# Down projection of the short token tiles on two column halves of the array

## The chip, the core and the metric

One core of a Trainium2 chip runs one program. The metric is the device time of the program in microseconds, the median of several executions; less is better. The engines named below are TensorE (PE; its weight loads are listed as PEld), VectorE (DVE), ScalarE (ACT), GpSimd (POOL) and SyncE (SP, which issues most DMAs).

## What is computed

A delta-rule attention over 4 batches, 8 heads, 768 tokens, whose output (4 x 768 tokens of 384 channels) goes through a mixture of 8 experts, of which each token uses one:

```python
# x: [4, 768, 384] from the attention; w1: [8, 384, 1024]; w2: [8, 1024, 384]
e = fresh_e if (s == 0 or local_gate[b, s] < 0.5) else prev_e
...
h = np.maximum(x[b, s] @ w1[e], 0.0)
out[b, s] = p[e] * (h @ w2[e])
```

The change concerns the last line, the down projection `h @ w2[e]`, for a few of the tokens.

## The kernel before

The first 440 us or so hold the attention, the routing and the mixture's expert 0 and place 1, issued in an order written out by hand. Then `Moe.rest` runs places 2 to 7: the experts other than 0, the fullest first. A place `e` has a fixed number of token slots, `CAPS[e]`, out of (480, 496, 480, 448, 416, 384, 384, 384), in tiles of 128, so that the last tile of a place can be shorter: 96 slots for place 2, 64 for place 3, 32 for place 4; places 5 to 7 have three full tiles.

Numbers are kept in two float16 parts, hi and lo, and a product is three matmuls: hi by hi, hi by lo, lo by hi.

One place goes as follows in the program, and each engine takes its instructions in this order.

- At the start the weights of the place after it are asked for: seven pieces (three of `w1`, pieces 0 to 2; four of `w2`, pieces 3 to 6), through four staging buffers on SP's queue. The tokens of the place after it are gathered on POOL (L490) and later transposed by a DMA (L842).
- Up projection: for each of 8 blocks `f` of 128 hidden channels, 9 matmuls into one of three PSUM banks `pt` (L502), with the weights as the stationary operand and the place's tokens as the columns that stream. ACT makes the hi part of `h` from the bank (`uphi`, L503), DVE a float32 copy (`upt`, L504), and DVE the lo part (L850).
- Down projection: for each token tile `j` of `m` tokens 24 matmuls (`downm`, L509) into one of two PSUM banks `po`. Here the tokens' hidden values are the stationary operand (128 channels by `m` tokens), and 384 output columns of `w2` stream. Then DVE scales the bank into a buffer `y` (`yo`, L510), and POOL scatters the rows to DRAM (L492).
- Between these, the weights of the place after it are split: ACT makes the hi part of a piece (`whi`, L485), DVE the lo part (`wlo`, L487). At tile `j` = 3 both parts of the last piece, 6, stand behind the tile's scaling. A lo part that is done frees a staging buffer, for which SP's next weight load waits.

Some work on the list of tokens that did not fit (L760 to L830) is put between tiles.

Of the kernel before, what the change touches and what calls it, by code (L numbers as in the profile page):

```python
"""Delta-rule attention followed by a top-1 mixture of experts with carried routing."""
# [13 lines left out]
class Buf:  # L15
    """a buffer of a pool, placed when its first instruction is issued"""
# [11 lines left out]
class Sched:  # L28
    """the instructions in program order, with what each reads, writes, writes a part of, and holds; issued in the order of ORDER.
    A function with a parameter gets the engine that ORDER names."""  # L30
# [19 lines left out]
class Attn:  # L50
    NKT=9; NKJ=9; NQC=2; NBD=2; GATE=1; NKF=4; NK16=2; NQV=3; NY=2; NCMP=3; NAM=1; NLX=2; NTT=1; NTX=1; NXC=1; NPO=2; NPK=1; NPT=3; AMG=()
    def __init__(s, ctx, tc, qv,k,beta,xs,wg,wl,lg):
        s.tc=tc; s.nc=nc=tc.nc; s.xs=xs
        s.qv_,s.k,s.beta=qv,k,beta
        s.NSTEP=k.shape[0]; s.NM=s.NSTEP//4
        s.wg,s.wl,s.lg=wg,wl,lg; s.sqrts=[]
        E=ctx.enter_context
        s.cp=E(tc.tile_pool(name="ac",bufs=1))
        s.pp=E(tc.tile_pool(name="ap",bufs=1,space=PSUM))
        T=lambda sh,dt,n:s.cp.tile(sh,dt,name=n)  # L60
        P=lambda n,sh,dt,nm:Pool_([T(sh,dt,f"{nm}{i}") for i in range(n)],nm)
        s.zsrc=T([128,1],F32,"zsrc")
        s.mask=T([128,32],F32,"mask")       # [(h,s),t]: 2^-6 where s<t
        s.KJ=P(s.NKJ,[128,2,8,128],F16,"KJ")       # token-major, head j of pair at column 64 j
        s.KT=P(s.NKT,[128,2,8,128],F16,"KT")       # [(j,d), z, u, (h,s)]
        s.QT=P(2,[128,2,2,8,128],F16,"QT")         # [(j,d), p, z, u, (h,t)] zero but for the heads of pair p
        s.QC=P(s.NQC,[128,2,8,2,32],F16,"QC")      # [(j,d), z, u, p, t]; the squares too
        s.bd=P(s.NBD,[128,32,128],F16,"bd")
        s.kf=P(s.NKF,[128,2,384],F32,"kf"); s.qv=P(s.NQV,[128,896],F32,"qv")
        s.bt=P(2,[128,32],F32,"bt")  # L70
        s.ss=P(2,[128,32],F32,"ss"); s.s0=P(1,[128,32],F32,"s0"); s.t0=P(1,[128,32],F32,"t0"); s.rr=P(2,[128,32],F32,"rr")
        s.k16=P(s.NK16,[128,2,2,384],F16,"k16")
        s.gt=P(1,[128,32,32],F32,"gt"); s.L=P(s.NLX,[128,1056],F32,"L"); s.X=P(s.NLX,[128,1056],F32,"X"); s.TT=P(s.NTT,[128,32,32],F32,"TT"); s.bs=P(1,[128,32],F32,"bs")
        s.ft=P(2,[128,256],F32,"ft"); s.mneg=T([128,1],F32,"mneg"); s.c64=T([128,1],F32,"c64")   # -2^-6 for the first 16 rows of a head, else 0
        s.TX=P(s.NTX,[128,16,32],F32,"TX"); s.XC=P(s.NXC,[128,2,16,32],F16,"XC"); s.GC=P(s.NXC,[128,2,32,16],F16,"GC"); s.QQ=P(1,[128,2,8,16],F16,"QQ")
        s.cmp=P(s.NCMP,[128,4,8,32],F16,"cmp"); s.am=P(s.NAM,[128,8,32],F32,"am")
        s.R=P(2,[128,4,48],F32,"R"); s.Rs=P(2,[128,2,4,48],F16,"Rs"); s.Us=P(2,[128,2,4,48],F16,"Us")
        s.y=P(s.NY,[128,2,2,384],F16,"y")
        s.Shp=P(3,[128,2,4,48],F16,"Sh"); s.Slp=P(3,[128,2,4,48],F16,"Sl")
        s.Sps=s.pp.tile([128,2,512],F32,name="Sps")  # L80
        s.po=Pool_([s.pp.tile([128,512],F32,name=f"po{i}") for i in range(s.NPO)],"po")
        s.pk=Pool_([s.pp.tile([128,512],F32,name=f"pk{i}") for i in range(s.NPK)],"pk")
        s.pt=Pool_([s.pp.tile([128,512],F32,name=f"pt{i}") for i in range(s.NPT)],"pt")
        if s.GATE:
            s.wc=T([128,3,9],F32,"wc"); s.wc16=T([128,2,3,9],F16,"wc16")
            s.xt=P(1,[128,12,128],F16,"xt")
    @staticmethod
    def blk(t,z,u,p): return t[:,p,z,u,:]
    def build(s,extra=(),post=None):
# [3 lines left out]
        # ---- constants  # L93
# [25 lines left out]
        # ---- program  # L119
# [57 lines left out]
        def K3(i,k16,k6,ii):  # L177
# [10 lines left out]
            # the keys without the zeros of the other head's rows  # L188
# [6 lines left out]
            g=s.pt()  # L195
# [14 lines left out]
        def T_(m):  # L210
            M=mac[m]; L=s.L(); X=s.X(); bs=s.bs(); TT=M["TT"]=s.TT(); gt=M["gt"]; b=M["b"]
            full=lambda t:t[:,0:1024].rearrange("p (a b)->p a b",a=32)
            dia=lambda t:t.rearrange("p (b r)->p b r",b=2)[:,:,0:512].rearrange("p b (j i)->p b j i",i=32)[:,:,:,0:16]     # both diagonal blocks: [p, block, j, i]
# [30 lines left out]
        def Q(i):  # L244
# [9 lines left out]
            for j in range(2):  # L254
                def qp(j=j):
                    q=slice(64*j,64*j+64); t=QT.t[q]; (a,_),(b,_)=t.ap[0],t.ap[1]
                    o=bass.AP(t.tensor,t.offset+32*j,[[a,64],[b+64,2],[128,16],[1,32]])      # the pair's columns lie 64 further in its own block
                    return o,QC.t[q].rearrange("r z u p c -> r p (z u) c")
                add(cp(qp),r=[QC],p=[QT]); D.setdefault('dq',[]).append(S.ops[-1])
# [20 lines left out]
        def Tc(i):  # L280
# [3 lines left out]
            # the lower left block of the inverse: - X22 G21 X11  # L284
# [30 lines left out]
        def online(i):  # L315
            D=st[i]; qv=D["qv"]; vb=lambda:qv.t[:,512:896].rearrange("p (u d) -> p u d",u=8); h_=i%2; y=D["y"]=s.y() if h_==0 else st[i-1]["y"]; KT,QT,KJ,bd=D["KT"],D["QT"],D["KJ"],D["bd"]
            for g in range(2):
                po=s.po(); pk=s.pk()
                psv=lambda po=po:po.t[:,0:384].rearrange("p (k u e) -> p k u e",k=2,u=4)      # U, y
                pkv=lambda pk=pk:pk.t[:,0:384].rearrange("r (u p e) -> r u p e",u=4,p=2)      # K S of both pairs  # L320
                bdv=lambda:bd.t.rearrange("p (k u) t -> p k u t",k=4)
                Rs=s.Rs(); Us=s.Us(); us=slice(4*g,4*g+4)
                if i>0:
                    HL=((0,(0,1)),(1,(0,)))           # the state's hi with both parts of k or q, its lo with the hi
# [71 lines left out]
        # program order of unplaced buffers does not matter: pools place them when scheduled  # L396
# [6 lines left out]
class Moe:  # L403
    CAPS=(480,496,480,448,416,384,384,384)            # slots of expert 0, then of the others, the fullest first
    SP=20; LOT=256                                    # expert 0 begins with up to LOT tokens of the first SP steps
    def __init__(s, ctx, tc, xs, lg, w1, w2, out):
        """xs [step, (b, t 32), d] in DRAM; lg [(b, t), step, logits and local logit] on chip; out [(b, t), d]"""
# [6 lines left out]
        s.NA=4*s.E+s.MO                                   # slot tiles: four of each place, then the overflow's  # L414
# [3 lines left out]
    def consts(s):  # L418
        """closures that make the constants, for the scheduler"""
        nc=s.nc; NS,E,SP=s.NS,s.E,s.SP; K=s.K  # L420
        s.ident=K([128,128],F16,"mident"); s.blk=K([128,128],F32,"blk")
        s.ones=K([128,128],F16,"ones"); s.tri=K([128,128],F16,"tri")       # tri [k,m]: 1 where k<m
# [25 lines left out]
        def f3():  # L448
# [6 lines left out]
            # key of a token: 8 (32 step + t) + 16, and 1..8 to be taken off  # L455
# [4 lines left out]
    # ---- pieces of the work  # L460
    def wsrc(s,e,k):
        """source of piece k of an expert's weights, and its shape: three of w1, four of w2"""
# [13 lines left out]
    def wv(s,t,k):  # L476
        """a piece's hi and lo, [p, hi|lo, a, b]"""
# [17 lines left out]
    def xtr(s,p,hl,m):  # L495
        """rows [m, hi|lo] -> [128 d, 6, m] in a bank"""
# [8 lines left out]
    def downm(s,po,h,W,fs,c,m):  # L505
        for f in fs:
            k=3+f//2
            for x,(a,b) in enumerate(((0,0),(0,1),(1,0))):
                s.nc.tensor.matmul(po[0:m],h(a,f)[:,c:c+m],s.wv(W[k],k)[:,b,f%2,:],start=(x==0 and f==0),stop=(x==2 and f==7))  # L509
    def yo(s,y,po,pv,m): s.nc.vector.tensor_scalar(y[0:m],po[0:m],pv[0:m],2.0**-26,op0=ALU.mult,op1=ALU.mult)  # L510
    # ---- routing, expert 0 and what place 1 starts from, as a part of the attention's schedule
    def graph(s,S,A):
# [3 lines left out]
        v=add  # L516
        # kept for the whole of the rest
# [14 lines left out]
        # weights of expert 0  # L532
# [16 lines left out]
        for z,(lo,hi) in enumerate(((0,SP),(SP,NS))):  # L549
# [15 lines left out]
            # a fresh choice where the gate, in float32, is below 0.5, and at the start  # L565
# [4 lines left out]
            # the last key so far: within a step, then over the steps  # L570
# [13 lines left out]
            # rank of a token among its expert's: the steps before, then the partitions before  # L584
            pr=A.pt(); prv=lambda pr=pr,n=n:pr.t[:,0:8*n].rearrange("p (e i) -> p e i",e=E); ptv=lambda pr=pr:pr.t[:,480:488]
            if z==0:
# [13 lines left out]
                # the others by their counts in the first steps, the fullest first: the place of each, the expert of each place, its slots  # L600
                EE=[128,E,E]; one=lambda a:a.unsqueeze(1).to_broadcast(EE); two=lambda a:a.unsqueeze(2).to_broadcast(EE)
                def f1():
# [3 lines left out]
                    V.tensor_tensor(pE,one(s.io[:,0:E]),two(s.ps),op=ALU.is_equal)       # [expert, place]  # L606
# [29 lines left out]
            if z==1:  # L636
                # a lot's second half also holds expert 0's of the first steps
# [7 lines left out]
            # softmax of the chosen expert, times 2^8, in two parts  # L645
# [9 lines left out]
            # the slots' tokens: one-hot products, 1[place] x 1[slot tile] values  # L655
# [23 lines left out]
            # the lot  # L679
# [32 lines left out]
        def f3():  # L712
            # rank, beyond the capacity, slot tile 4 place + rank / 128
# [11 lines left out]
        # place 1, and what place 2 starts from  # L725
# [48 lines left out]
    # ---- places 1.. and what did not fit  # L774
    def rest(s,A):
# [19 lines left out]
        def load(e):  # L795
            """closures: hi, lo of each piece"""
# [13 lines left out]
        def ov1():  # L810
            # tiles of 128 ranks from the capacity on, of each expert: their number, where they start
# [14 lines left out]
            # the expert of each such tile  # L826
# [17 lines left out]
        for e in range(2,E):  # L844
# [10 lines left out]
            for j in range(nj):  # L855
                m=min(128,n-128*j); po=pso()[:,0:384]; y=s.f32(yo())[:,0:384]; a=4*e+j
                s.downm(po,lambda z,f:h(z,f,n),W[e],range(8),128*j,m)
                s.yo(y,po,s.pv[:,a:a+1],m); s.scatter(y,s.so[:,a:a+1],m)
# [31 lines left out]
# the instructions of the attention and of the start of the mixture, in the order of issue; a letter names the engine where several can do it  # L890
# [111 lines left out]
def _layout(q, k, v, beta):  # L1002
    """tokens in steps of 32; batch 2 p + j, head u, chunk 4 m + c; q and v side by side"""
# [31 lines left out]
```

## Time and profile before

| | |
|---|---|
| time, median of three runs | 613.91 us (614.52, 611.40, 613.91) |
| span of the profiled execution, first to last instruction | 614.3 us |
| the profiled execution's own time | 614.52 us: the other two times are below its span |
| mean granted TensorE clock | 0.864 of full speed over the span |
| busy share of the span: PE, PEld | 77%, 60% |
| DVE, ACT, POOL | 85%, 56%, 55% |
| PE, tenths, last 12 of 40 slices | 999999999993 |
| granted clock there | 999999999997 |

A slice is 15.4 us long, and 9 stands for 90% or more. The shares mix stages with different limits: DVE has the largest share over the whole span, while in the last 12 slices PE is full and DVE's digits are 785868597650. Places 2 to 7 lie in these slices. A matmul is pipelined, and the length shown for one contains the run through the array; what one costs in a stream is read from the distance of starts.

### The profile page before, as it was taken

What the parts mean: (1) busy time and instruction counts of PE and PEld (TensorE: products, weight loads), DVE (VectorE), ACT (ScalarE), POOL (GpSimd) and SP (SyncE); (2) the same over time, 40 slices, a digit from 0 to 9 for tenths busy, and PEclk for the clock granted to TensorE, in tenths of its full rate; (3) what the DMA queues carried; (4) which work ended last, traced back from release to release, by engine and by line L of the source; (5) the groups of instructions that cost most, each with busy time, mean ns of one, the idle gap of its engine ahead of it and who ended that gap; (6) DMA issues with size and microseconds to landing.
All of it is one profiled execution on the core that took longest, in us unless ns stands there. A gap on an engine that the chain in (4) does not pass through costs nothing. (4 is left out here: it accounts for less than half of the span.)

```text
span 614.3 us, 19858 instructions
## 1 busy us (share of the span) xinstructions
PE 473.4 (77%) x8023; PEld 366.8 (60%) x8023; DVE 520.8 (85%) x1163; ACT 346.8 (56%) x745; POOL 340.8 (55%) x474
## 2 busy tenths in 40 slices
PE   0131677677789668687878769799999999999993
PEld 0131676677678667686777766654656555666661
DVE  7999998999899899989989998699785868597650
ACT  7567697678778777777878743213160605154220
POOL 7837686657667675757556764378843232414201
PEclk9998587588867777869867578799999999999997
DMA  5777777589899997797775617272567465666600
GB/s 191 129 163 119 165 99 131 93 162 169 126 164 165 131 145 127 122 161 158 121 191 118 127 40 253 70 227 89 145 209 211 127 194 170 187 162 221 120 16 29
DMA packets 244703, 88.23 MB, mean 144 GB/s; under 512 B 221651, under 2 KB 236047, under 8 KB 244608
## 3 DMA queue, kind: packets, MB, share of 16 engines
q1 hardware_dynamic: 241056, 76.87, 61.0%
q0 software_dynamic: 3552, 10.06, 5.2%
q8 instruction: 64, 1.05, 0.8%
q14 instruction: 31, 0.25, 0.2%
HBM read 46.34 MB, written 10.05 MB: 92 GB/s over the span
## 5 line engine op out<-in xcount | busy, mean ns | idle before, releaser
L502 PE MATMUL pt<-bd,KT 128*128 128x384 f16 (+4 forms) x432 | 92.0, 346 | 2.6 <-DVE tx L768 1.1
L502 PEld LDWEIGHTS <-KT 128*128 128x128 f16 x576 | 57.7, 102 | 44.3 <-issue 6.4
L201 PE MATMUL pt<-QC,KT 128*128 128x64 f16 x576 | 29.1, 222 | 41.7 <-DVE QC L126 28.8
L509 PE MATMUL po<-KJ,QT 128*128 128x384 f16 (+2 forms) x336 | 55.5, 326 | 0.0
L201 PEld LDWEIGHTS <-KT 128*128 128x128 f16 x576 | 26.9, 117 | 42.5 <-issue 39.6
L503 ACT ACTIVATE QT<-pt 128x384 f16<-128x384 f32 (+2 forms) x32 | 16.7, 526 | 61.9 <-PE pt L502 42.7
L509 PE MATMUL po<-KJ,L 128*128 128x384 f16 (+2 forms) x208 | 50.7, 326 | 0.0
L503 ACT ACTIVATE L<-pt 128x256 f16<-128x256 f32 (+4 forms) x40 | 18.2, 463 | 55.8 <-PE pt L502 46.1
L509 PEld LDWEIGHTS <-QT 128*128 128x128 f16 (+2 forms) x336 | 33.9, 101 | 21.1 <-issue 0.3
L329 PEld LDWEIGHTS <-KT 128*128 128x128 f16 x552 | 35.5, 117 | 16.6 <-issue 7.9
L504 DVE TENSOR_SCALAR qv<-pt 128x384 f32<-128x384 f32 (+4 forms) x56 | 33.4, 599 | 11.2 <-ACT L L503 5.5
L336 PEld LDWEIGHTS <-QT 128*128 128x128 f16 x1104 | 41.4, 107 | 1.0 <-issue 0.8
L350 PE MATMUL po<-Rs,bd 128*128 128x48 f16 x576 | 27.4, 195 | 17.7 <-DMA bd<-cmp 7.0
L492 POOL DMA_INDIRECT out_dram<-y,so x9 | 11.2, 1245 | 50.8 <-DVE y L510 50.5
L266 PE MATMUL pt<-QC,KT 128*128 128x64 f16 x576 | 31.4, 223 | 8.2 <-DVE QC L251 3.1
L329 PE MATMUL pk<-Sh,KT 128*128 128x96 f16 x368 | 30.1, 241 | 7.9 <-DVE R L341 6.5
L341 DVE SCALAR_TENSOR_TENSOR R<-pk,qv 64x192 f32<-64x192 f32 x92 | 32.4, 352 | 3.4 <-PE pk L329 1.9
L232 POOL TENSOR_TENSOR X<-X,ft 128x30 f32<-128x30 f32 (+7 forms) x75 | 31.5, 420 | 5.9
L350 PEld LDWEIGHTS <-bd 128*128 128x128 f16 x576 | 22.2, 104 | 20.2 <-issue 12.0
L509 PE MATMUL po<-KJ,X 128*128 128x384 f16 (+2 forms) x104 | 33.9, 326 | 0.0
L362 PE MATMUL Sps<-Us,KJ 64*128 64x48 f16 x1104 | 29.2, 195 | 5.4 <-DVE Us L353 4.1
L292 PE MATMUL pt<-XC,bd 128*128 128x16 f16 x576 | 21.0, 191 | 15.7 <-DVE XC L126 6.5
(316 smaller groups left out, 1503.4 us busy)
## 6 DMA issues: line engine op xcount, KB each, us to landing
KT<-in_moe_w_dram SPq DMA_DIRECT2D x24, 512.0 KB, 4.5
qv<-in_qv_dram SPq DMA_DIRECT2D x24, 448.0 KB, 4.7
KT<-in_moe_w_dram SPq DMA_DIRECT2D x20, 384.0 KB, 3.3
xs<-y SPq DMA_DIRECT2D x12, 384.0 KB, 4.4
KJ<-in_moe_w_dram SPq DMA_DIRECT2D x12, 384.0 KB, 4.6
kf<-in_k_dram SPq DMA_DIRECT2D x10, 384.0 KB, 4.2
bd<-cmp SPq DMA_DIRECT2D x58, 64.0 KB, 3.7
KJ<-k SPq DMA_DIRECT2D x65, 48.0 KB, 3.6
```

Source lines behind the costliest of these rows:

```text
L201: nc.tensor.matmul(gv[:,u,:],KT.t[:,z,u,:],KC.t[:,y,u].rearrange("r p t -> r (p t)"),start=(x==0),stop=(x==2),skip_group_check=True)
L232: eng.tensor_tensor(x[:,:,j+1:,0:k],x[:,:,j+1:,0:k],tv,op=ALU.subtract)
L266: nc.tensor.matmul(gv[:,u,:],KT.t[:,z,u,:],QC.t[:,y,u].rearrange("r p t -> r (p t)"),start=(x==0),stop=(x==2),skip_group_check=True)
L329: for uu in range(4): nc.tensor.matmul(pkv()[:,uu],KT.t[:,z,4*g+uu,:],S_.t[:,:,uu,:],start=(y_==0 and z==0 and uu==0),stop=(y_==1),skip_gr ...
L336: for p in range(2): nc.tensor.matmul(psv()[:,1,uu,:],s.blk(QT.t,z,4*g+uu,p),S_.t[:,p,uu,:],start=(y_==0 and z==0 and uu==0 and p==0),stop ...
L341: add(lambda R=R,pkv=pkv,us=us,q=q,p=p:nc.vector.scalar_tensor_tensor(R.t[q],pkv()[q,:,p,:],-2.0**-10,vb()[q,us,:],op0=ALU.mult,op1=ALU.ad ...
L350: for uu in range(4): nc.tensor.matmul(psv()[:,0,uu,:],bdv()[:,a_,4*g+uu,:],Rs.t[:,b,uu,:],start=(i==0 and b==0 and a_==2 and uu==0),stop= ...
L362: nc.tensor.matmul(s.Sps[:,p,48*u:48*u+48],KJ.t[q,a_,u,:],Us.t[q,b,uu,:],start=(i==0 and u==0 and b==0 and a_==0),stop=False,skip_group_ch ...
L502: for k in range(3): s.nc.tensor.matmul(ps,s.wv(W[k],k)[:,a,0,128*f:128*f+128],xT[:,3*b+k,:],start=(x==0 and k==0),stop=(x==2 and k==2))
L503: def uphi(s,h,ps): s.nc.scalar.activation(h,ps,AF.Relu,scale=2.0**-6)
L504: def upt(s,t,ps): s.nc.vector.tensor_scalar(t,ps,0.0,2.0**-6,op0=ALU.max,op1=ALU.mult)
L509: s.nc.tensor.matmul(po[0:m],h(a,f)[:,c:c+m],s.wv(W[k],k)[:,b,f%2,:],start=(x==0 and f==0),stop=(x==2 and f==7))
```

## The change

Tiles of at most 64 tokens (the fourth of place 3, with 64, and the fourth of place 4, with 32) go through a new function, `down2`. The stationary operand of such a tile has 64 or 32 columns and so needs at most half of the array's columns. `down2` puts it on both halves, columns 0 to 63 and 64 to 127 (`tile_position=(0,64*g)`), and streams output columns 0 to 191 through the one and 192 to 383 through the other. Per tile there are 48 matmuls of 192 columns with 48 weight loads, where there were 24 of 384 columns with 24 loads. The results of the halves lie in partitions 0 and up, and 64 and up, of the same PSUM bank: ACT copies the second half into `y`, and DVE scales the first half from the bank and the second in place.

```diff
+    def down2(s,po,h,W,c,m,y,pv):
+        for f in range(8):
+            k=3+f//2
+            for x,(a,b) in enumerate(((0,0),(0,1),(1,0))):
+                for g in range(2):
+                    s.nc.tensor.matmul(po[64*g:64*g+m,0:192],h(a,f)[:,c:c+m],s.wv(W[k],k)[:,b,f%2,192*g:192*g+192],start=(x==0 and f==0),stop=(x==2 and f==7),skip_group_check=True,tile_position=(0,64*g))
+        s.nc.scalar.copy(y[0:m,192:384],po[64:64+m,0:192])
+        s.nc.vector.tensor_scalar(y[0:m,0:192],po[0:m,0:192],pv[0:m],2.0**-26,op0=ALU.mult,op1=ALU.mult)
+        s.nc.vector.tensor_scalar(y[0:m,192:384],y[0:m,192:384],pv[0:m],2.0**-26,op0=ALU.mult,op1=ALU.mult)
...
-                s.downm(po,lambda z,f:h(z,f,n),W[e],range(8),128*j,m)
-                s.yo(y,po,s.pv[:,a:a+1],m); s.scatter(y,s.so[:,a:a+1],m)
+                if m>64:
+                    s.downm(po,lambda z,f:h(z,f,n),W[e],range(8),128*j,m); s.yo(y,po,s.pv[:,a:a+1],m)
+                else: s.down2(po,lambda z,f:h(z,f,n),W[e],128*j,m,y,s.pv[:,a:a+1])
+                s.scatter(y,s.so[:,a:a+1],m)
```

The lines that follow in the program move by 10 or more. Nothing else in the program is changed.

On ACT, at the end of place 3 (`KJ` and `KT` hold weight pieces, L485 makes their hi parts, L503 evacuates the next place's first bank; `QC` is the tile's `y`):

```order
 L485 ACTIVATE KJ_75<-KT_85 128x768
 L485 ACTIVATE KJ_80<-KT_86 128x768
+L517 COPY QC_96<-po_150 64x192
 L485 ACTIVATE KJ_79<-KT_88 128x768
 L503 ACTIVATE L_117<-pt_155 128x416
```

The copy stands ahead of the hi part of piece 6 (`KJ_79`), which had no instruction of this tile ahead of it on ACT.

On ACT, at the end of place 4, with the same names:

```order
 L485 ACTIVATE KJ_81<-KT_89 128x768
 L485 ACTIVATE KJ_82<-KT_85 128x768
+L517 COPY QC_95<-po_150 32x192
 L485 ACTIVATE KJ_83<-KT_86 128x768
 L503 ACTIVATE QT_93<-pt_154 128x384
```

The same has moved: `KJ_83` is that place's piece 6.

On DVE, at the end of place 3, before, with the semaphores that each row waits for (`Activation` is ACT, `DMAHW` a load, `DMASW` a scatter):

```order
L510 TENSOR_SCALAR QC_95<-po_151,pvs 128x384 [waits DMASW1_49,PE_49]
L487 SCALAR_TENSOR_TENSOR KJ_80<-KT_86,KJ_80 128x768 [waits DMAHW7_49,Activation_49]
L510 TENSOR_SCALAR QC_96<-po_150,pvs 64x384 [waits DMASW2_49,PE_49]
L487 SCALAR_TENSOR_TENSOR KJ_79<-KT_88,KJ_79 128x768 [waits DMAHW0_49,Activation_49]
L504 TENSOR_SCALAR qv_105<-pt_155 128x416 [waits Activation_49]
```

and there now (L520 is L510 of before):

```order
L520 TENSOR_SCALAR QC_95<-po_151,pvs 128x384 [waits DMASW1_49,PE_49]
L487 SCALAR_TENSOR_TENSOR KJ_80<-KT_86,KJ_80 128x768 [waits DMAHW7_49,Activation_49]
L518 TENSOR_SCALAR QC_96<-po_150,pvs 64x192 [waits DMASW2_49,Activation_49]
L519 TENSOR_SCALAR QC_96<-QC_96,pvs 64x192
L487 SCALAR_TENSOR_TENSOR KJ_79<-KT_88,KJ_79 128x768 [waits DMAHW0_49,Activation_49]
L504 TENSOR_SCALAR qv_105<-pt_155 128x416 [waits Activation_49]
```

One instruction became two, and the first of them waits for ACT in place of PE. On PE the same place has 48 pairs of a load and a matmul where 24 stood.

## The prediction

> **What bounds the kernel now.** I read the busy time by stage first, to see which engine limits the stretch in which the change lies. Columns after the stretch and its length: busy time and count of PE (matmuls), PEld (weight loads), DVE, ACT, POOL, then the granted TensorE clock.
>
> ```profile
> span 614.3 us, 19858 instructions
> ...
> 351.00:443.00 92.00, 78.60 (x729) 54.63 (x725) 81.00 (x170) 26.74 (x52) 58.69 (x45) 0.91 0.47 135
> 443.00:604.00 161.00, 160.88 (x1012) 94.46 (x1010) 113.65 (x193) 54.40 (x83) 48.95 (x41) 1.00 0.57 159
> 604.00:614.30 10.30, 0.00 (x0) 0.00 (x0) 0.54 (x1) 0.00 (x0) 0.98 (x1) 0.66 0.06 19
> ```
>
> From 443 us to 604 us, places 2 (its end) to 7 of the mixture, PE is busy 160.88 of 161.00 us at clock 1.00, DVE only 113.65. After it comes 10 us of ending that the change does not touch. So a microsecond taken off PE in this stretch comes off the whole, as long as no other engine becomes late.
>
> Second, the two tiles that the change rewrites, the fourth of place 3 (64 tokens) and the fourth of place 4 (32 tokens). Their stretches run from the first matmul of the tile to the first of the next place:
>
> ```profile
> 499.66:503.68 4.02, 4.02 (x25) 2.56 (x25) 3.31 (x8) 0.00 (x0) 1.20 (x1) 1.00 0.28 77
> 528.82:532.83 4.01, 4.01 (x27) 2.25 (x25) 0.92 (x2) 0.00 (x0) 1.45 (x1) 1.00 0.76 245
> ```
>
> Each takes as long as a tile of 128 tokens: 4.0 us, all of it PE. Nothing else waits there to be uncovered, so 8.03 us of the execution is what the change can work on.
>
> Third, the timeline of PE, for what a matmul costs in a stream (start, length of the group, its instructions; a group's length holds the run-out of its last matmul, so the pitch is read from start to start).
>
> ```profile
> 372.40 2.13 PE L502 MATMUL pt<-KT,KT 128*128 128x256 f16 x18
> 374.37 0.49 PE L509 MATMUL pt<-KJ,L 128*128 128x384 f16 x2
> ...
> 592.02 11.86 PE L509 MATMUL po<-KJ,QT 128*128 128x384 f16 x72
> L509 PE MATMUL po<-KJ,QT 128*64 128x384 f16 x24 | 4.1, 327 | 0.0
> ```
>
> 18 matmuls of 256 columns take 374.37-372.40 = 1.97 us, 109.4 ns each. 72 of 384 columns take 11.86-0.33 = 11.53 us for 71 steps, 162.4 ns each, and the 24 with 64 tokens fill their 4.02 us the same way: the columns streamed count, the tokens do not. The slope is (162.4-109.4)/128 = 0.414 ns per column, so 192 columns come to 109.4-64*0.414 = 82.9 ns.
>
> **The change part by part.**
>
> *Removed:* two times 24 matmuls of 384 columns: 2*24*162.4 ns = 7.80 us of PE.
>
> *Added:* two times 48 matmuls of 192 columns, in pairs, one on each column half. No column half is used apart from the other in the trace of before, so their cost is bounded. Lower end: the two of a pair stream at the same time, 24 steps of 82.9 ns, 1.99 us per tile, 3.98 us for both. Upper end without other harm: one after the other, 48 steps, 3.98 us per tile, 7.96 us for both. The nearest row is the state update of the attention, where two row halves alternate instruction by instruction (64*128 is the part of the array used):
>
> ```profile
> 302.93 0.33 PE L329 MATMUL pk<-Sl,KT 128*128 128x96 f16 x4 [1.39 <-DVE Sl L367]
> 303.19 0.54 PE L362 MATMUL Sps<-Us,KJ 64*128 64x48 f16 x24
> 303.67 0.47 PE L372 MATMUL po<-Us,bd 128*128 128x48 f16 x12
> 303.98 0.56 PE L336 MATMUL po<-Sh,QT 128*128 128x48 f16 x16
> 304.38 0.60 PE L385 MATMUL pt<-wc,xt 128*128 128x9 f16 x18
> ```
>
> On the whole array 48 columns cost (303.98-303.67)/12 = 26 ns and (304.38-303.98)/16 = 25 ns. The 24 on row halves would need 0.60 us one after the other; they took 303.67-303.19 = 0.48 us, and in that lies also the return to the whole array. Two halves do run at the same time there. I take the lower end, 3.98 us: gain 7.80-3.98 = 3.82 us. What is not the same is that column halves need two streams through the same rows; this doubt goes into the chances.
>
> *Weight loads:* 48 per tile in place of 24. Their price while hidden is nothing; the cover is the matmul ahead.
>
> ```profile
> L509 PEld LDWEIGHTS <-QT 128*128 128x128 f16 x288 | 28.2, 98 | 18.9
> L509 PEld LDWEIGHTS <-QT 128*64 128x64 f16 x24 | 2.6, 110 | 1.5 <-issue 0.3
> L509 PEld LDWEIGHTS <-L 128*32 128x32 f16 x16 | 1.5, 97 | 1.0
> 499.66 3.71 PEld L509 LDWEIGHTS <-QT 128*64 128x64 f16 x24 [0.32 <-issue]
> 503.68 2.40 PEld L502 LDWEIGHTS <-KT 128*128 128x128 f16 x15 [0.30 <-issue]
> ```
>
> 24 loads of 110 ns lie within the 4.02 us that the matmuls fill, on the same 128 rows; none of them shows in the pitch of 162.4 ns. The state update gets through two loads and two matmuls per 40 ns, so two loads per 82.9 ns fit. The Trainium skill, page "TensorE: Matmul & The Clock Gate", section Part 3, says that a weight load overlaps matmuls in flight only where its row group differs; by that, neither of the old tiles could have had its loads hidden, and this trace disagrees (110 ns loads, no gap). By the rule no load of the new tiles would hide either, and the sum would be that of the third rival below.
>
> *Change of the array's shape:* the last two rows show that loads stop for 0.30 us at both ends of the 64-token tile: its stretch of 4.02 us is 24 steps (3.90 us) plus 0.12 us. The old tile already used a part of the columns, so this is paid now and stays. Zero, with 0.1 us per tile either way as bounds.
>
> *Evacuation:* one DVE instruction per tile (0.6 us) becomes an ACT copy, then two on DVE, and the first of these waits for ACT (the rows with their waits are shown with the change). ACT runs in order, so the hi part of the next place's last weight piece (L485) now queues behind a copy that waits for the tile's end; the lo part (L487, DVE) waits for that, and behind it stands the first evacuation (L504) of the next place, whose first matmuls are on PE meanwhile. The timeline of before at the second tile:
>
> ```profile
> 532.57 0.33 PE L509 MATMUL po<-KJ,X 128*32 128x384 f16 x1
> 532.93 0.60 DVE L510 TENSOR_SCALAR QC<-po,pvs 32x384 f32<-32x384 f32 x1 [3.20 <-PE po L509]
> 533.47 0.94 DVE L487 SCALAR_TENSOR_TENSOR KJ<-KT,KJ 128x768 f16<-128x768 f32 x1
> 534.50 0.49 ACT L503 ACTIVATE QT<-pt 128x384 f16<-128x384 f32 x1 [12.00 <-PE pt L502]
> 535.03 0.56 DVE L504 TENSOR_SCALAR qv<-pt 128x384 f32<-128x384 f32 x1 [0.62 <-ACT QT L503]
> ...
> 544.54 4.06 PE L509 MATMUL po<-KJ,QT 128*128 128x384 f16 x24
> ...
> 547.25 0.56 DVE L850 TENSOR_TENSOR QT<-qv,QT 128x384 f16<-128x384 f32 x1
> ```
>
> And from the groups by line (count, busy us and mean ns, then idle time before them), what the new instructions are sized by:
>
> ```profile
> L352 ACT ACTIVATE Us<-po 128x192 f16<-128x192 f32 x48 | 15.7, 328 | 20.1 <-PE po L350 19.6
> L485 ACT ACTIVATE KJ<-KT 128x768 f16<-128x768 f32 x20 | 15.9, 837 | 11.9 <-DMA KT<-in_moe_w_dram 9.6 <-DVE KJ L487 2.3
> L504 DVE TENSOR_SCALAR ft<-pt 128x224 f32<-128x224 f32 x8 | 3.1, 388 | 3.6 <-ACT L L503 3.0 <-PE pt L502 0.5
> ```
>
> Counted from the tile's end (532.90): copy to 0.4 (328 ns and a start), hi part to 1.2 (837 ns), the two scalings on DVE to 1.2 (at most 388 ns each), lo part 0.94 to 2.15. L504 started at 535.03-532.90 = 2.13 before. So the chain just fits into the 0.62 us for which DVE idled. Then DVE runs without a pause to 547.81, and PE needs its last product at the 24th matmul, 544.54+23*0.1624 = 548.28: another 0.47 us before PE stalls. The copy could be 0.5 us slower and still cost nothing. At the first tile DVE is behind anyway, with work on the overflow list that does not move forward with PE:
>
> ```profile
> 502.12 0.95 DVE L487 SCALAR_TENSOR_TENSOR KJ<-KT,KJ 128x768 f16<-128x768 f32 x1
> 503.79 0.61 DVE L510 TENSOR_SCALAR QC<-po,pvs 64x384 f32<-64x384 f32 x1 [0.71 <-PE po L509]
> 506.03 0.59 DVE L504 TENSOR_SCALAR qv<-pt 128x416 f32<-128x416 f32 x1 [0.76 <-ACT L L503]
> 507.61 0.59 DVE L504 TENSOR_SCALAR qv<-pt 128x416 f32<-128x416 f32 x1 [0.36 <-ACT L L503]
> 509.19 0.59 DVE L504 TENSOR_SCALAR qv<-pt 128x416 f32<-128x416 f32 x1 [0.36 <-ACT L L503]
> ```
>
> With PE done 1.9 us earlier (about 501.8), DVE is free at 503.0, scales to 503.8, makes the lo part to 504.7, and L504, due at 506.03-1.9 = 504.1, is 0.6 us late; the next two pauses of 0.36 us take that up. Price 0, upper bound 0.5 us per tile.
>
> *POOL and SP:* the scatter waits for DVE's second scaling and goes out at most 0.6 us later against the tile's end; SP's weight load into the staging buffer that the lo part frees moves with it. Both are hidden by the place that follows (503.68 to 532.83, 29 us), at whose end the pieces are first used; without that cover it would be the 0.6 us.
>
> **Sum.** -7.80+3.98 = -3.82 us. The profiled execution must be the 614.52 us one, since the other two runs are shorter than its span of 614.3 us; it would become 610.7 us. It is 0.6 us above the median of 613.91, and so the median becomes 610.1 us. That is 0.62% less, while about 0.5% (3.07 us) is the least that a measurement of this kernel can tell from no change.
>
> **The rivals.**
>
> 1. *The halves take turns.* Then the instructions are there and the gain is not: 48*82.9 ns = 3.98 us against 3.90 us per tile, +0.16 us, 614.1 us. For it: no row of before has two streams on the same rows. Against: the row halves above.
>
> 2. *PE gains, and part of it is given back in the next place,* because the chain copy, hi part, lo part, L504 is longer than I count. At the upper bounds, 0.5 us at each of two places: 611.1 us. For it: DVE has no pause from 535.03 to 547.81. Against: 0.47 us of room.
>
> 3. *Slower: weights of one half cannot be loaded while either half computes.* Place: each of the 96 loads. Price: 48*(82.9+110) = 9.26 us for the 64-token tile, 48*(82.9+97) = 8.64 us for the other, against 7.80: +10.1 us, 624.0 us. It is slower by over 0.5% from (3.07-0.16)/96 = 30 ns of uncovered load per matmul on. For it: the loads double, and every one aims at a half that is in use. Against: the loads of before on rows in use. The rule of the Trainium skill above would give this case; its page "TensorEngine Tiling (Array Packing)", section Tiling Modes, says instead that different tiles load and multiply in parallel, which is the forecast.
>
> **How the numbers follow.** Forecast 0.80, rival 1 0.09, rival 2 0.06, rival 3 0.05. The three runs of before lie within 611.4 and 614.52 us, so a median may sit 1.6 us off: the forecast's own range is 608.5 to 611.7. The range given takes in rivals 1 and 2: 608.5 to 614.2; rival 3 and the tails are left out. With that spread the forecast shows as faster by over 0.5% in about three of four cases, 0.59; rival 2 adds 0.02. Slower is rival 3 and a tail of rival 1, 0.06. The rest, 0.33, is within 0.5%.
>
> **What would show it.** Right: the two stretches last 2.1 us each, with matmuls of a pair starting within some nanoseconds of each other and pairs 83 ns apart; PE busy without a gap to the end of place 7, which comes 3.8 us earlier. Rival 1: stretches of 4.1 us, starts 83 ns apart. Rival 2: short tiles and an idle PE, released by DVE, at the start of the down projection of places 4 or 5. Rival 3: stretches near 9 us and loads that start only when a matmul has ended. Wrong altogether would be a different granted clock after 443 us, or a place that waits for its weights.

## The result and the profile after

The changed kernel takes 609.09 us (median of 6 runs, 607.97 to 609.85), the kernel before 613.48 us beside it (6 runs, 611.4 to 617.05). The ratio is 0.993, with a 95% interval of 0.9905 to 0.9954: 2.8 to 5.8 us less. The forecast was 610.1 us; the likeliest case came true.

The traces say where it came from. First the busy time by stage of before, cut at the first matmul of place 2 and at the end of PE's work (columns as in the prediction: stretch, length, busy time and count of PE, PEld, DVE, ACT, POOL, granted clock, DMA share, GB/s):

```profile
0.00:443.39 443.39, 312.96 (x7016) 272.58 (x7017) 407.01 (x971) 292.41 (x662) 291.05 (x433) 0.82 0.72 141
443.39:603.88 160.49, 160.49 (x1009) 94.20 (x1007) 113.17 (x192) 54.40 (x83) 48.79 (x40) 1.00 0.57 159
```

The same view of after; its last two rows are the two rewritten tiles, which were 4.02 and 4.01 us:

```profile
span 608.0 us, 19960 instructions
...
0.00:441.07 441.07, 311.62 (x7015) 269.99 (x7016) 406.56 (x971) 292.04 (x662) 291.67 (x433) 0.85 0.71 142
441.07:597.73 156.66, 156.66 (x1058) 93.28 (x1055) 113.17 (x194) 54.89 (x85) 48.79 (x40) 1.00 0.58 163
597.73:608.00 10.27, 0.00 (x0) 0.00 (x0) 0.62 (x1) 0.00 (x0) 0.98 (x1) 0.68 0.06 19
...
497.35:499.45 2.10, 2.10 (x49) 1.96 (x48) 2.00 (x7) 0.00 (x0) 0.00 (x0) 1.00 0.04 14
524.59:526.68 2.09, 2.09 (x51) 1.93 (x49) 0.92 (x2) 0.00 (x0) 1.44 (x1) 1.00 0.71 222
```

The stretch that PE bounds went from 160.49 to 156.66 us, 3.83 less. The tiles account for all of it: 4.02-2.10 and 4.01-2.09 are 3.84 us. PE has no idle time in the stretch in either kernel (156.66 of 156.66). The two spans differ by 6.3 us, but 2.3 us of that lies ahead of place 2, which the change does not touch: in the ten traces of this study place 2 starts anywhere from 439.22 to 443.39 us. A comparison of whole times carries that scatter; the stretch does not. One more profile of the unchanged kernel (label before_again, 611.97 us, no edit) shows it:

> The kernel before, unchanged, for a second trace. Expected: its time is its span and 1.75 us, as in the executions of the changed kernel, so that the first profiled execution took about 616.0 us and not 614.52; from the first matmul of place 2 to the end of the last one 160.5 us as in the first trace (in the changed kernel 156.7); the start of place 2 lies anywhere from 439 to 444 us. Rival (the stretch from place 2 on varies by itself by a microsecond or more, so that the 3.8 us are not all the change's): a length outside 160.2 to 160.8 us.

```profile
439.22:599.72 160.50, 160.50 (x1010) 94.22 (x1007) 113.16 (x192) 54.58 (x83) 48.38 (x40) 1.00 0.56 159
```

Place 2 starts 4.2 us earlier than in the first trace, and the stretch is the same within 0.01 us. So the experiments below are read by this stretch and by the tile's own stretch, and a single profile of each is enough for tenths of a microsecond there.

Inside the tiles, PE's timeline of after (start, length of the group with its run-out, its instructions):

```profile
497.35 2.17 PE L516 MATMUL po<-KJ,QT 128*64 128x192 f16 x48
499.45 3.87 PE L502 MATMUL pt<-bd,KT 128*128 128x416 f16 x21
...
524.59 0.34 PE L516 MATMUL po<-KJ,L 128*32 128x192 f16 x4
524.77 0.25 PE L516 MATMUL po<-KJ,X 128*32 128x192 f16 x2
524.85 0.33 PE L516 MATMUL po<-KJ,L 128*32 128x192 f16 x4
...
526.34 0.33 PE L516 MATMUL po<-KJ,L 128*32 128x192 f16 x4
526.50 0.25 PE L516 MATMUL po<-KJ,X 128*32 128x192 f16 x2
526.68 0.50 PE L502 MATMUL pt<-bd,KT 128*128 128x384 f16 x2
```

Per block `f` there are six matmuls, a group of four and a group of two. From the first group of four to the last, seven blocks later, are 526.34-524.59 = 1.75 us, 0.25 us per six matmuls. Within it a group of four starts 0.16 to 0.18 us before the next group and a group of two 0.08 us: three steps of 82 to 83 ns, two matmuls in each. In the single records the two of a pair start 3 to 4 ns apart.

### The profile page after: what moved, and what is told of

The parts are those of the page before. It is cut to its first block, busy times and chain, and to the rows that moved or that the text cites. A ratio compares the mean times of both kernels' runs of the same rounds, so it can differ in the third digit from the quotient of the medians.

```text
span 608.0 us, 19960 instructions
## 1 busy us (share of the span) xinstructions
PE 468.3 (77%) x8071; PEld 363.3 (60%) x8071; DVE 520.4 (86%) x1165; ACT 346.9 (57%) x747; POOL 341.4 (56%) x474
## 5 line engine op out<-in xcount | busy, mean ns | idle before, releaser
L509 PE MATMUL po<-KJ,QT 128*128 128x384 f16 (+1 forms) x312 | 51.5, 326 | 0.0
L509 PE MATMUL po<-KJ,L 128*128 128x384 f16 (+1 forms) x192 | 46.8, 326 | 0.0
L503 ACT ACTIVATE QT<-pt 128x384 f16<-128x384 f32 (+2 forms) x32 | 16.7, 526 | 50.5 <-PE pt L502 29.8
L509 PEld LDWEIGHTS <-QT 128*128 128x128 f16 (+1 forms) x312 | 31.3, 100 | 19.7
L503 ACT ACTIVATE L<-pt 128x256 f16<-128x256 f32 (+4 forms) x40 | 18.2, 462 | 43.1 <-PE pt L502 30.0
L504 DVE TENSOR_SCALAR qv<-pt 128x384 f32<-128x384 f32 (+4 forms) x56 | 33.3, 598 | 9.7 <-ACT QT L503 4.4
L336 PEld LDWEIGHTS <-QT 128*128 128x128 f16 x1104 | 39.2, 104 | 1.7 <-issue 1.4
L372 PE MATMUL po<-Us,bd 128*128 128x48 f16 x576 | 27.6, 198 | 7.1 <-DVE Us L353 7.1
```

What stands on the lines that cost most here:

```text
L336: for p in range(2): nc.tensor.matmul(psv()[:,1,uu,:],s.blk(QT.t,z,4*g+uu,p),S_.t[:,p,uu,:],start=(y_==0 and z==0 and uu==0 and p==0),stop ...
L503: def uphi(s,h,ps): s.nc.scalar.activation(h,ps,AF.Relu,scale=2.0**-6)
L504: def upt(s,t,ps): s.nc.vector.tensor_scalar(t,ps,0.0,2.0**-6,op0=ALU.max,op1=ALU.mult)
```

## The experiments

**Do the halves gain because they run side by side? (g_outer)** The same 48 matmuls, but one half after the other.

```
         for f in range(8):
-            k=3+f//2
-            for x,(a,b) in ...:
-                for g in range(2):
+        for g in range(2):
+            for f in range(8):
+                k=3+f//2
+                for x,(a,b) in ...:
                     s.nc.tensor.matmul(po[64*g:64*g+m,0:192], ...)
```

> The same 48 matmuls per tile, but all 24 of the first column half and then all 24 of the second. Theory (a matmul starts in program order, and two run at the same time only when the next one in the program uses the other half): only the one pair at the border overlaps, 47 steps of 82.5 ns plus 0.12 us for the change of shape, so each short tile lasts 4.0 us against 2.1 us in the changed kernel and 4.0 us before; the whole gain is lost, ratio to before 1.000. Rival (matmuls are taken out of order from a window, so that the halves find each other): tiles stay at 2.1 us and the ratio at 0.993. Second rival (the gain comes from the evacuation or from the shorter matmuls, not from two at a time): tiles stay well below 4.0 us.

The tiles and the stretch of g_outer, in the view by stage:

```profile
440.64:600.64 160.00, 160.00 (x1058) 96.63 (x1055) 113.45 (x194) 55.08 (x85) 49.16 (x40) 1.00 0.56 159
...
496.92:500.70 3.78, 3.78 (x49) 3.63 (x49) 3.31 (x8) 0.00 (x0) 0.95 (x1) 1.00 0.18 55
525.84:529.59 3.75, 3.75 (x51) 3.59 (x49) 0.91 (x2) 0.00 (x0) 1.45 (x1) 1.00 0.73 245
```

and PE's timeline of the second tile, where the first half has run 18 matmuls, two of `L` and one of `X` for each block `f`:

```profile
527.34 0.33 PE L516 MATMUL po<-KJ,L 128*32 128x192 f16 x2
527.50 0.25 PE L516 MATMUL po<-KJ,X 128*32 128x192 f16 x1
527.50 0.41 PE L516 MATMUL po<-KJ,L 128*32 128x192 f16 x4
```

612.81 us against 612.46 us, ratio 1.0013 (0.999 to 1.0035): the gain is gone but for 0.5 us of the stretch (160.00 against 160.49 before), with the same instructions, loads and evacuation. So it comes from two halves streaming at once, and from nothing else in the edit. One thing is off. One after the other, with the border shared by one pair, is 47 steps; 3.75 us less 0.12 us for the change of shape is 44 steps of 82.5 ns. In the trace the second half starts at 527.50, beside the 21st matmul of the first half (the one of `X`) and ahead of three that stand before it in the program. Away from there, one matmul per step, the starts are 82 to 83 ns apart, as the pairs are in the changed kernel.

**How far do matmuls overtake? (g_middle, block6, block12)** The same matmuls in blocks of 3, 6 and 12 per half.

```
g_middle:  for f in range(8):  for g in range(2):  for x,(a,b) in ...:
block6:    for f0 in range(0,8,2):  for g in range(2):  for f in range(f0,f0+2):  for x,(a,b) in ...:
block12:   for f0 in range(0,8,4):  for g in range(2):  for f in range(f0,f0+4):  for x,(a,b) in ...:
```

> Blocks of three matmuls on one half, then three on the other (the loop over the halves lies outside that over the hi and lo products). Theory of starts in program order: the last matmul of a block and the first of the next one share a step, so 48 matmuls take 48-15 = 33 steps of 82.5 ns, 2.72 us, plus 0.12 us: 2.84 us per short tile. Rival (out of order within a window): 2.1 us. Rival (halves must be in lockstep pairs throughout, or a change of half costs something): 4.0 us or more.

> Blocks of six. With a window of four matmuls 26 steps, 2.15 us plus 0.12: 2.27 us per short tile (window of three 27 steps, 2.35 us; of six 24 steps, 2.10 us). Rival (program order of starts): 41 steps, 3.50 us.

> Blocks of twelve matmuls on one half, then twelve on the other. Theory now (TensorE starts the first matmul whose half is free among the next few that have not started; the run with 24 on each half, whose halves met for about 4 of 48 steps, says about four matmuls with their loads): counted step by step with a window of four, 48 matmuls take 36 steps of 82.5 ns, 2.97 us, plus 0.12 us: 3.09 us per short tile (window of three 39 steps, 3.34 us; of six 30 steps, 2.60 us). Rival (program order of starts, one shared step at each border): 45 steps, 3.83 us. Rival (a window that holds the tile): 2.1 us.

Their tiles in the view by stage, g_middle (608.14 us), block6 (609.65 us) and block12 (610.75 us):

```profile
495.58:497.69 2.11, 2.11 (x49) 1.97 (x49) 2.01 (x7) 0.00 (x0) 0.00 (x0) 1.00 0.05 19
522.83:524.92 2.09, 2.09 (x51) 1.93 (x48) 0.92 (x2) 0.00 (x0) 1.44 (x1) 1.00 0.74 216
```

```profile
524.12:526.38 2.26, 2.26 (x51) 2.10 (x48) 0.91 (x2) 0.00 (x0) 1.45 (x1) 1.00 0.59 214
```

```profile
524.51:527.63 3.12, 3.12 (x51) 2.96 (x49) 0.91 (x2) 0.00 (x0) 1.45 (x1) 1.00 0.72 234
```

Blocks of three cost nothing (2.09 us). Had every matmul waited for the start of the one ahead of it in the program, the tile would have taken 2.84 us; that theory of mine fell. Less 0.12 us and divided by 82.5 ns, blocks of 3, 6, 12 and 24 take 24, 26, 36 and 44 steps. A window of the next four matmuls, which fills up as soon as one has started, and out of which any whose half is free may start, gives all four counts. Its size was drawn from the blocks of 24; the 2.27 and 3.09 us of block6 and block12 were expected from it before they ran. With their loads these are eight instructions, and the runs cannot tell which of the two is counted. The Trainium skill, page "TensorE: Matmul & The Clock Gate", section Part 3, says that matmuls keep program order in start and end; on one set of columns no run here contradicts that, but for the starts of matmuls on different column halves these four do (2.09 us for blocks of three, where starts in order would give 2.84).

**How much room has the evacuation? (copies6)** The ACT copy of the second half is issued six times.

```
-        s.nc.scalar.copy(y[0:m,192:384],po[64:64+m,0:192])
+        for _ in range(6): s.nc.scalar.copy(y[0:m,192:384],po[64:64+m,0:192])
```

> The ACT copy of the second half is issued six times instead of once in each of the two short tiles (same data), which makes the chain copy, hi part, lo part, first evacuation of the next place about 5*0.22 = 1.1 us longer. Theory (the chain is covered by DVE's pauses in place 4 and by 0.39 us of room in place 5): the first L504 of place 5 comes about 1.0 us later against the tile's end, and PE stalls 0.6 to 0.7 us at the end of the first down projection tile of place 5; in place 4 DVE's pauses take it up and PE stalls 0 to 0.1 us. Rival (the chain is on PE's path at once): 1.1 us lost at each place, 2.2 us. Rival (the chain does not matter): no stall.

First the chain at the end of place 4 in after's timeline: ACT, then DVE, then the PE group that starts place 5's down projection.

```profile
526.79 0.31 ACT L517 COPY QC<-po 32x192 f32<-32x192 f32 x1 [11.69 <-PE po L516]
527.01 0.84 ACT L485 ACTIVATE KJ<-KT 128x768 f16<-128x768 f32 x1
...
527.14 0.41 DVE L518 TENSOR_SCALAR QC<-po,pvs 32x192 f32<-32x192 f32 x1 [1.63 <-ACT QC L517]
527.47 0.30 DVE L519 TENSOR_SCALAR QC<-QC,pvs 32x192 f32<-32x192 f32 x1
527.88 0.96 DVE L487 SCALAR_TENSOR_TENSOR KJ<-KT,KJ 128x768 f16<-128x768 f32 x1
528.94 0.56 DVE L504 TENSOR_SCALAR qv<-pt 128x384 f32<-128x384 f32 x1
...
541.17 0.56 DVE L860 TENSOR_TENSOR QT<-qv,QT 128x384 f16<-128x384 f32 x1
...
538.39 4.88 PE L509 MATMUL po<-KJ,QT 128*128 128x384 f16 x29
```

DVE's last product (L860, the lo part, which was L850) is ready at 541.17+0.56 = 541.73; PE needs it at the 24th matmul, 538.39+23*0.1624 = 542.13. So 0.4 us of room is left (0.39 unrounded). Now copies6 (612.55 us): its stretch, and in its timeline the copies, the first L504, and on PE the first matmul of place 5 and the three places where PE waits.

```profile
442.55:600.37 157.82, 157.19 (x1058) 93.09 (x1055) 113.01 (x194) 57.91 (x95) 50.38 (x40) 1.00 0.57 161
```

```profile
528.32 2.03 ACT L517 COPY QC<-po 32x192 f32<-32x192 f32 x6 [10.89 <-PE po L516]
...
532.00 0.55 DVE L504 TENSOR_SCALAR qv<-pt 128x384 f32<-128x384 f32 x1
...
528.18 0.50 PE L502 MATMUL pt<-bd,KT 128*128 128x384 f16 x2
...
534.39 0.48 PE L502 MATMUL pt<-bd,KT 128*128 128x384 f16 x2 [0.17 <-DVE qv L504]
...
537.65 0.48 PE L502 MATMUL pt<-bd,KT 128*128 128x384 f16 x2 [0.17 <-DVE qv L504]
...
544.76 1.47 PE L509 MATMUL po<-KJ,QT 128*128 128x384 f16 x8 [0.29 <-DVE QT L860]
```

Six copies took 2.03 us, (2.03-0.31)/5 = 0.34 us for each further one, more than the 0.22 us that I expected, after which the hi part starts behind a single copy. In the trace each further copy waits for the semaphore that the copy before it raises. But that is not shown to be the whole reason: the three copies of the run with quarters below write different columns and have no such wait, and they do not overlap either (0.72 us together, 0.23 us each). L504 comes 532.00-528.18 = 3.82 us after place 5's first matmul, 2.26 in after: 1.56 us later. Less 0.39 us of room, PE should lose 1.17 us; the stretch is 157.82-156.66 = 1.16 us longer. PE waits twice for L504 to free a bank and once for the last product; each idle time shown hides the 0.16 us by which a group's length runs past its last step, so they are 0.33, 0.33 and 0.45 us, 1.1 together. So the chain counted in the prediction (copy, hi part, lo part, L504, place 5) is the one that binds once it is late, and its room is 0.39 us. At the end of place 3 the six copies made L504 1.2 us later too, and PE has no idle time there.

**Does it go on with narrower parts? (quarters, thirds)** The 32-token tile on four parts of 96 output columns, and on three of 128; the 64-token tile as in after.

```
+    def down4(s,po,h,W,c,m,y,pv):      # down3: range(3), 128 columns each
+        for f in range(8):
+            k=3+f//2
+            for x,(a,b) in enumerate(((0,0),(0,1),(1,0))):
+                for g in range(4):
+                    s.nc.tensor.matmul(po[32*g:32*g+m,0:96], ..., tile_position=(0,32*g))
+        for g in range(1,4): s.nc.scalar.copy(y[0:m,96*g:96*g+96],po[32*g:32*g+m,0:96])
...
+                elif m<=32: s.down4(po,lambda z,f:h(z,f,n),W[e],128*j,m,y,s.pv[:,a:a+1])
```

> The tile of 32 tokens on four column quarters, 96 output columns each, 96 matmuls and 96 loads, with three ACT copies; the tile of 64 tokens stays on halves. Theory (as many matmuls at a time as there are free column parts): 24 steps of 96*0.414+2.9 = 42.6 ns, 1.02 us plus 0.11: the tile lasts 1.13 us against 2.09, the total 0.96 us less than the changed kernel. Rival (instructions get through at no more than the state update's one load and matmul per 12.5 ns): 24 steps of 50 ns, 1.31 us. Rival (two streams at most): 2.1 us.

> The tile of 32 tokens on three column parts of 32, with 128 output columns each: 72 matmuls and 72 loads, two ACT copies; the tile of 64 tokens stays on halves. Theory on the two pauses in the run with quarters (the first 46 matmuls ran at 42.5 ns per four, then TensorE had no instructions: 192 instructions in 2.1 us, 11 ns each, with some 92 waiting at the start): 144 instructions over 24 steps of 128*0.414+2.9 = 55.9 ns, 1.34 us, fit into 92 plus what arrives, so the tile lasts 1.34+0.11 = 1.45 us without a pause, 0.64 us less than on halves. Rival (the pause is due to the fetch of the next block of instructions, whatever their rate): a pause of 0.4 us or more stays, 1.9 us. Total against before: about -4.5 us, ratio 0.9925; it can't be told from the changed kernel by its time.

Quarters: 609.76 us, ratio 0.9956 (0.9937 to 0.9975). By stage the tile and the stretch, and then the timeline of the tile on PE, with the three ACT copies behind it:

```profile
523.92:526.14 2.22, 1.58 (x100) 1.19 (x97) 0.91 (x2) 0.00 (x0) 1.45 (x1) 1.00 0.70 223
440.40:597.19 156.79, 156.14 (x1105) 92.54 (x1103) 112.93 (x194) 55.33 (x87) 48.98 (x40) 1.00 0.56 163
```

```profile
523.92 0.27 PE L525 MATMUL po<-KJ,L 128*32 128x96 f16 x8
524.01 0.22 PE L525 MATMUL po<-KJ,X 128*32 128x96 f16 x4
...
524.81 0.23 PE L525 MATMUL po<-KJ,X 128*32 128x96 f16 x2 [0.20 <-issue]
...
525.73 0.30 PE L525 MATMUL po<-KJ,L 128*32 128x96 f16 x8 [0.44 <-issue]
...
526.26 0.72 ACT L526 COPY QC<-po 32x96 f32<-32x96 f32 x3 [11.83 <-PE po L525]
```

I expected 1.13 us and got 2.22. The first 46 matmuls run as expected, 42.5 ns per four; then PE stands still twice, waiting for nothing that the profile shows, and so do the weight loads. 96 loads and 96 matmuls in 2.1 us are 11 ns per instruction. That instructions arrive too slowly fits this, and the run with thirds bears on it, but the cause of the pauses stays open. The transfers that the trace lists for instructions do not end them: in the tile there is one, of 16 KB, which starts at 525.13 us, after the first pause, and takes 1.0 us, so that it lands after the second one has ended at 525.73.

Thirds: 607.81 us (606.62 to 611.01) against 612.39 us, ratio 0.9918 (0.9884 to 0.9953). Its tile and stretch by stage, then two groups of the tile on PE and a row of the weight loads at the start of place 5:

```profile
526.22:527.72 1.50, 1.50 (x75) 1.40 (x73) 0.92 (x2) 0.00 (x0) 1.17 (x1) 1.00 0.73 296
442.71:598.91 156.20, 156.20 (x1081) 92.68 (x1079) 112.98 (x194) 55.17 (x86) 49.05 (x40) 1.00 0.56 163
```

```profile
526.90 0.28 PE L525 MATMUL po<-KJ,L 128*32 128x128 f16 x6
...
527.07 0.33 PE L525 MATMUL po<-KJ,L 128*32 128x128 f16 x6
...
528.02 0.10 PEld L502 LDWEIGHTS <-KT 128*128 128x128 f16 x1 [0.21 <-issue]
```

Three parts stream at once, 56 ns per three, with no pause inside the tile: 1.50 us where 1.45 was expected. The pause of 0.4 us or more that the other theory expected is not there. But after 46 matmuls, as many as ran ahead of the first pause of quarters, the starts change: up to there the three of a step start 3 to 4 ns apart, and from then on 13 to 28 ns, at 57 ns per three. Two of the groups above show it: six matmuls that start on the same pitch last 0.28 us before and 0.33 us after. So both runs change at the same count of instructions; what changes there, no run here shows. Of the 0.59 us saved against two halves the stretch keeps 0.46, since at the start of place 5 a load comes late. By the trace this is the best version of all. By its time it cannot be told from the changed kernel (0.9918 against 0.993, with intervals that overlap).

## Why the prediction was right, step by step

- *Removed and added matmuls, -3.82 us:* right; -3.84 us in the tiles. The 82.9 ns per pair, drawn from the slope of two row widths, was 82.5. Rival 1 (halves take turns) is out, by the tiles themselves and by g_outer, which is what it would have looked like. The doubt about two streams through the same rows is settled: a column half costs the other nothing (82.5 ns per step for a pair, and for one alone in g_outer).
- *Weight loads hidden:* right. The groups of after, on PEld (count, then busy us and mean ns of one, then the idle time ahead of them):

```profile
L516 PEld LDWEIGHTS <-QT 128*64 128x64 f16 x48 | 2.0, 110 | 0.3 <-issue 0.3
L516 PEld LDWEIGHTS <-L 128*32 128x32 f16 x32 | 1.4, 97 | 0.0
```

  48 loads of 110 ns lie in a tile of 2.10 us that 24 steps of matmuls fill. Rival 3 (loads of a half wait for the halves) needed 9 us. The rule of the Trainium skill behind it, page "TensorE: Matmul & The Clock Gate", section Part 3, that a load overlaps with matmuls in flight only on another row group, does not hold here: all of these are on the same 128 rows. The same section also lets a load for a background weight buffer be pulled ahead of matmuls, and that would allow what the trace shows; no run here tells the buffer apart.
- *Change of the array's shape, 0:* right; 24*82.5 ns = 1.98 us, and 0.12 us remain of the 2.10 as of the 4.02 before, with the same 0.3 us pause of the loads.
- *Evacuation, 0:* right, and each step of the chain within 0.2 us. From the tile's end (526.50+0.25 = 526.75) the copy ends at 0.35 us (0.4 counted), the hi part at 1.10 (1.2), the scalings at 1.02 (1.2), the lo part at 2.09 (2.15), and L504 starts at 2.19 (2.13 before). The room of 0.47 us became 0.4. Rival 2 is the right mechanism at a price of zero; copies6 shows where the price begins. At the end of place 3, L504 came 502.11-499.45 = 2.66 us after place 4's first matmul, 2.35 before: 0.3 us late and not 0.6, taken up there.
- *POOL and SP, nothing:* nothing seen against it, since PE has no gap to the end of place 7. It was not varied.
- *The profiled execution's own time:* wrong, here and in the table of times before. I took it for the 614.52 us run, since the two others are shorter than the span. In every later run whose span is listed the time is the span and 1.7 us (609.75 and 608.0 in after, 611.97 and 610.3 in before_again), so the first profile, with a span of 614.3 us, must belong to an execution of about 616.0 us that is none of the three. I carried the same 3.82 us to the median, so the forecast did not suffer, but the profile stood 2.1 us above the median and not 0.6.
- *The median, 610.1:* 1.0 us too high, within its own range of 608.5 to 611.7. The runs of before drew 613.48 us this time, 0.43 lower than the three shown; the rest, 0.6 us, lies within the scatter ahead of place 2, where the traces differ by 4.2 us, and was not traced further. The 3.8 us themselves do not rest on these medians.

## What to carry to other kernels

Where an engine is busy without a gap, read the gain from that stretch alone: there 3.82 us could be told to 0.02 us, while six whole times of one kernel lay up to 5.7 us apart. A stationary operand of at most half the columns leaves the other half free to work at the same time: give it other output columns, alternate the halves in short blocks (three matmuls cost nothing here, six 0.17 us per tile), and look at what the split evacuation does to the first evacuation of the next stage. Before widening the evacuation, work out how late the last consumer may be; here that left 0.39 us, and of 1.17 us beyond it 1.16 were paid.

## What the runs showed that I had not expected

- Matmuls of different column halves overtake each other within a window of about four matmuls: 24, 26, 36 and 44 steps for blocks of 3, 6, 12 and 24.
- Four column parts of 96 columns run at 42.5 ns per four for 46 matmuls and then stop twice (0.20 and 0.44 us), three of 128 columns run at 56 ns per three without a stop, but less closely together after the same 46; why is open.
- Six ACT copies into the same place start 0.34 us apart, three into different columns 0.24 us, while the hi part of a weight piece follows a copy after 0.22 us, before the copy has ended.
